# Attention probabilities of the first block: transposed by a float32 matmul with diag(1/sum) in place of a DMA, and a longer search for the order of the instructions

## The chip, the core and the metric

The kernel runs on one core of one Trainium2 chip. The metric is the device time of one execution in microseconds (us). The core has five engines with a queue each: TensorE (PE; its weight loads are listed apart as PEld), VectorE (DVE), ScalarE (ACT), GpSimd (POOL) and SyncE (SP), which here issues all transfers of the 16 DMA engines.

## What is computed

```python
# q, k, v: (4 batches, 12 heads, 448 positions, 64), float32
scores = q @ k.T / sqrt(64), causal mask
attn = exp(scores - max); attn = attn / (sum(attn) + 1e-9)
x = (attn @ v), heads side by side          # (1792, 768)
h = x @ w_in                                # w_in (768, 2048), float64
g = h * sigmoid(1.702 * h)
out = g @ w_out                             # w_out (2048, 768), float64
```

The inputs w_in and w_out are float64, 12.6 MB each. Results are float32.

## The kernel before

**Numbers in two halves.** Nearly every operand of a matmul is held as two float16 numbers, a high part and a remainder, and each product is three matmuls (high x high, high x remainder, remainder x high). The helper `scaled` makes a high part (L472 on ScalarE, L474 on VectorE), `rest` the remainder (L477, VectorE only). The weights are read as raw float64 words and made float32 by integer operations in `to_f32` (L566, L574, L588, L599), scaled by the largest column norm (`gram`, `gram_max` at L628, `norm_scale` at L439 to L453) and then split into halves by `split`, into `wib` (w_in, 8 slices) and back into `wob` (w_out, 16 pieces).

**Blocks and units.** Each batch of 448 positions is 7 chunks of 64 queries and is cut into a block of 4 chunks and a block of 3, so there are 8 blocks. A block has 6 units, each of two heads side by side: the 128 partitions are 64 queries of either head. In batch 0 the q and k of six units are float32 and turned by TensorE with an identity (`turn`, L866, `k_unit32`, `q_unit32`), so their scores are float32 matmuls. For each chunk `chunk` takes scores from PSUM, masks them and finds the maximum (L1085, VectorE), and ScalarE takes the exponential and the sum (L1099) into the tile `z`. GpSimd or VectorE adds 1e-9 (L1157), VectorE takes the reciprocal (L1163), and `p_pair` writes z times 1/sum as high part and remainder into `p16`. When all chunks of the unit are there, one DMA (L1173) transposes all of `p16` into `PT`, 128x128 at a time, and `pv` (L1191) multiplies with v. After every second unit the result is split into `xT`.

**The MoE part.** `moe(n)` runs over 8 slices of w_in (`h_slice`): matmuls of xT and wib into one of three PSUM buffers `ps_h`, tanh (L1282), product (L1287), split into `gT`. Then `out_tile` multiplies 128 rows of gT with w_out (L1325) and stores them. The matmuls of a slice come in two halves, over units 0 to 2 and 3 to 5.

**Order.** Nothing runs in the order of the source. `add` collects each operation with the tiles that it reads and writes, its cost on each engine that may run it (the first engine named is preferred, another takes it when it has nothing else ready), and a due time. `order` simulates the engines, sorts again and again with random noise on the finishing times, keeps the best, and the instructions are issued in that order. Each engine's queue then runs strictly in its order.

Of the kernel before, what the change touches and what calls it, by code (L numbers as in the profile page):

```python
# [11 lines left out]
F32 = mybir.dt.float32  # L12
# [3 lines left out]
ALU = mybir.AluOpType  # L16
# [10 lines left out]
TUNE = dict(  # L27
    large=2,
    raw=(['W11', 'W11', 'V1', 'V1', 'W13', 'W15', 'W9', 'V0'], ['W11', 'W13', 'W15', 'V1', 'W15', 'V0', 'V0', 'V1']),
    tiny=True,  # L30
    win=(2, 4),
    slack=5.13,
    cuts={0: (0, 4, 7), 1: (0, 4, 7), 2: (0, 4, 7), 3: (0, 4, 7)},
    wi=(-21.7, 11.6),
    wo=(38.54, 116.08),
# [16 lines left out]
    wi2=2.63,  # L52
    dv0=-29.57,
    early=3,
)

SEED = 2
# [2 lines left out]
class Ops:  # L60
# [24 lines left out]
    def add(self, costs, fn, r=(), w=(), prio=0.0, dma=0.0):  # L85
        deps = set()
        for key in r:
            if key in self.wrote:
                deps.add(self.wrote[key])
        for key in w:  # L90
            if key in self.wrote:
                deps.add(self.wrote[key])
            deps.update(self.read.get(key, ()))
        me = len(self.ops)
        for key in r:
            self.read.setdefault(key, []).append(me)
        for key in w:
            self.wrote[key] = me
            self.read[key] = []
        deps.discard(me)  # L100
        self.ops.append((costs, fn, sorted(deps), prio, dma))

    ROUNDS, STEPS, SPREAD = 300, 6, (0.0, 0.0, 1.0, 3.0, 8.0)

    def order(self):
        rnd = Random(SEED)
# [188 lines left out]
def act(n, psum=False, ap=0, acc=0, rate=0.833):  # L295
    return {"ACT": (rate * n + (52 if psum else 94) + 93 * (ap + acc)) / 1e3}


def dve(n, ap=0, rate=1.042):
    return {"DVE": (rate * n + 68 + 61 * ap) / 1e3}  # L300
# [7 lines left out]
def pool(n, rate=1.885):  # L308
    return {"POOL": (rate * n + 220) / 1e3}
# [3 lines left out]
def kernel(  # L313
# [11 lines left out]
    B, H, S, D = q.shape  # L325
    DM, DFF = w_in.shape
    P = 128
# [19 lines left out]
    def bufs(n, shape, dt, name, pool=cp):  # L347
        return [pool.tile(shape, dt, name=f"{name}{i}") for i in range(n)], Ring(n)
# [14 lines left out]
    PT, PT_r = bufs(2, [P, NPT, 2, P], F16, "PT")  # L363
# [4 lines left out]
    p16, p16_r = bufs(2, [P, NPT, 2, P], F16, "p16")  # L368
# [8 lines left out]
    ps_h, ps_h_r = bufs(3, [P, 512], F32, "ps_h", pp)  # L377
# [7 lines left out]
    add = ops.add  # L385
# [14 lines left out]
    def by(e):  # L400
        return nc.gpsimd if e == "POOL" else nc.vector
# [7 lines left out]
    def halves(out, lhsT, rhs, start, stop):  # L409

        for o in range(0, P, 64):
            nc.tensor.matmul(out[o : o + 64], lhsT[:, o : o + 64], rhs, start=start, stop=stop)  # L412
# [56 lines left out]
    def scaled(e, dst, src, sc):  # L469

        if e == "ACT":
            nc.scalar.activation(out=dst, in_=src, func=AF.Copy, scale=sc)  # L472
        else:
            nc.vector.tensor_scalar(out=dst, in0=src, scalar1=sc, scalar2=None, op0=ALU.mult)  # L474

    def rest(dst, src, sc, hi):
        nc.vector.scalar_tensor_tensor(out=dst, in0=src, scalar=sc, in1=hi, op0=ALU.mult, op1=ALU.subtract)  # L477
# [355 lines left out]
    ident = cp.tile([P, P], F32, name="ident")  # L833
    ident_keys = ["ident"]
# [190 lines left out]
    def q_unit(n, u, prio):  # L1025
        b, c0, c1 = blocks[n]
        if f32(b, u):
            return q_unit32(n, u, prio)
        ni = c1 - c0
        if u % 2 == 0:  # L1030
            q_pair(n, u, prio)
        t, m = qT_r.next(), u % 2
        stale[t] = True
        add(
            Ops.turned(2 * ni),
            lambda e: nc.sync.dma_start_transpose(out=qT[t][:, : 2 * ni], in_=q16[:, m * 256 * ni : (m + 1) * 256 * ni]),
            [("q16", m, g) for g in range(4)], [("qT", t)], prio - TUNE["tr"], dma=2 * Ops.ROWS * ni,
        )
        return (qT[t][:, : 2 * ni].rearrange("p (c g) t -> p g c t", g=2), ("qT", t)) + bst[b]["c", n]
# [65 lines left out]
    def z_of(i):  # L1105
        return zt[:, z_at[i] : z_at[i] + i // 2 + 1]

    def z_keys(i):
        return [("z", e) for e in range(z_at[i], z_at[i] + i // 2 + 1)]

    def p_pair(i, pi, at, r, r_key, prio):
# [13 lines left out]
            zs + [r_key] + keys[0], keys[1], prio,  # L1125
        )

    def unit(n, u, prio):
        b, c0, c1 = blocks[n]
        ni = c1 - c0  # L1130
        w = 64 * ni
        qt, qt_key, c, c_key = q_unit(n, u, prio - TUNE["dq"])
        pi = PT_r.next()


        places = [(i, J) for i in range(c0, c1) for J in range(i // 2 + 1)]
        if c0 == 0:
            places.sort(key=lambda x: x[1])
        where = {x: at for at, x in enumerate(places)}
        vt, v_keys = bst[b]["v16", u]  # L1140
        vb = u % 2
        ps = ps_v[:, vb]
        pp_i = p16_r.next()
        for i0 in range(c0 - c0 % 2, c1, 2):
            run = range(max(i0, c0), min(i0 + 2, c1))
            ls, l_key = col("l", 3, 2)
            rs, r_key = col("r", 3, 2)
            joint = [run] if sum(64 * (i + 1) for i in run) <= 512 else [[i] for i in run]
            got = [x for y in joint for x in scores_of(n, u, y, qt, qt_key, prio)]
            for a, i in enumerate(run):  # L1150
                chunk(i, *got[a], c, c_key, ls[:, a : a + 1], (l_key, a), prio)
            ln = len(run)
            ls, rs = ls[:, :ln], rs[:, :ln]
            l_keys = [(l_key, a) for a in range(ln)]
            add(
                tiny(),
                lambda e, ls=ls: by(e).tensor_scalar(  # L1157
                    out=ls, in0=ls, scalar1=1e-9, scalar2=2.0**-14, op0=ALU.add, op1=ALU.mult
                ),
                [], l_keys, prio,  # L1160
            )
            add(
                dve(6 * ln), lambda e, ls=ls, rs=rs: nc.vector.reciprocal(rs, ls), l_keys, [r_key], prio  # L1163
            )
            for a, i in enumerate(run):
                at = [where[i, J] for J in range(i // 2 + 1)]
                assert at == list(range(at[0], at[-1] + 1, at[1] - at[0] if at[1:] else 1))
                p_pair(i, pp_i, at, rs[:, a : a + 1], r_key, prio)
        ne = len(places)
        all_keys = [("PT", pi)]  # L1170
        add(
            Ops.turned(2 * ne),
            lambda e: nc.sync.dma_start_transpose(  # L1173
                out=PT[pi][:, :ne].rearrange("p a g t -> p (a g) t"),
                in_=p16[pp_i][:, :ne].rearrange("p a g w -> p (a g w)"),
            ),
            [("p16", pp_i, x, g) for x in range(ne) for g in range(2)], all_keys, prio - TUNE["tr"],
            dma=2 * Ops.ROWS * ne,
        )
        terms = []  # L1180
        for J in range((c1 - 1) // 2 + 1):
            first = max(c0, 2 * J)
            at = [where[i, J] for i in range(first, c1)]
            step = at[1] - at[0] if len(at) > 1 else 1
            assert at == list(range(at[0], at[-1] + 1, step))
            terms += [(J, first, slice(at[0], at[-1] + 1, step), gv, gp) for gv, gp in ((0, 0), (0, 1), (1, 0))]

        def pv(e):
            for t, (J, first, at, gv, gp) in enumerate(terms):
                for j in range(2):  # L1190
                    nc.tensor.matmul(  # L1191
                        ps[64 * j : 64 * j + 64, 64 * (first - c0) : w],
                        vt[:, gv, J, j, :],
                        PT[pi][:, at, gp, 64 * j : 64 * j + 64],
                        start=(t == 0),
                        stop=(t == len(terms) - 1),
                    )

        add(
            {"PE": sum((64 * (c1 - t[1]) / 2.4 + 5) for t in terms) / 1e3}, pv, v_keys + all_keys, [("PV", vb)], prio,  # L1200
        )
        if vb == 0:
            return
        pv_keys = [("PV", 0), ("PV", 1)]
        x = n % 2
        hi, lo = (xT[x][:, g, u - 1 : u + 1, :w] for g in range(2))
        keys = [[("xT", x, u - a, g) for a in range(2)] for g in range(2)]
        add(
            act(2 * w, psum=True),
            lambda e: scaled("ACT", hi, ps_v[:, :, :w], 2.0**-14),  # L1210
            pv_keys, keys[0], prio,
        )
        add(
            dve(2 * w),
            lambda e: rest(lo, ps_v[:, :, :w], 2.0**-14, hi),
            pv_keys + keys[0], keys[1], prio,
        )
# [236 lines left out]
```

## Time and profile before

| | |
|---|---|
| Runs | 614.44, 616.70, 617.17 us, median 616.7 |
| Profiled execution | 616.57 us |
| Its span, first to last instruction | 614.9 us |
| TensorE busy | 566.6 us, 92% |
| VectorE busy | 419.9 us, 68% |
| ScalarE busy | 359.5 us, 58% |
| GpSimd busy | 95.3 us, 16% |
| Mean granted TensorE clock | 0.975 |

Busy time is the time in which at least one instruction of the engine ran. A granted clock of 1.00 is TensorE's full 2.4 GHz, 0.50 is 1.2 GHz. A wait is put down to the operation that came last.

### The profile page before, as it was taken

The page shows a single profiled execution, that of the slowest core. Times are in us where ns is not written, and L with a number is a line of the kernel's source. Part 1 is how long each engine was busy: PE and PEld are TensorE (multiplying, and loading weights), DVE is VectorE, ACT ScalarE, POOL GpSimd, SP SyncE. Part 2 cuts the span into 40 slices and gives each one's busy share as a digit, 9 for nine tenths or more (in the row PEclk, how much of TensorE's full clock was granted, in tenths as well). Part 3 has the DMA queues.
Part 4 walks back from the last instruction along what each step waited for, and adds up shares of the span by engine and source line. Part 5 has one row for each costly group of instructions (what it writes and reads, how often), then busy time and mean ns, then how long its engine had stood idle before and what let it go on. Part 6 is the DMA issues. An engine that isn't in the chain of part 4 may idle for free.

```text
span 614.9 us, 22331 instructions
## 1 busy us (share of the span) xinstructions
PE 566.6 (92%) x9502; PEld 503.8 (82%) x9502; DVE 419.9 (68%) x1117; ACT 359.5 (58%) x830; POOL 95.3 (16%) x251
## 2 busy tenths in 40 slices
PE   4667689888999999999998999999999999999997
PEld 4455368766699989987897879998899999889986
DVE  4999999998978789996588885886685213102300
ACT  6987797788857666775677665875454123102310
POOL 2222210123212011421111422211010000000000
PEclk9786899999999999999999999999999999999999
DMA  9999999949699979899876998884870500000000
GB/s 302 234 276 278 307 186 306 254 133 197 104 163 166 162 127 152 150 172 193 154 114 129 143 176 164 137 120 95 152 126 3 100 15 2 2 27 29 3 27 27
DMA packets 226435, 86.18 MB, mean 140 GB/s; under 512 B 207136, under 2 KB 216096, under 8 KB 226336
## 3 DMA queue, kind: packets, MB, share of 16 engines
q1 hardware_dynamic: 226336, 84.76, 68.0%
q8 instruction: 74, 1.21, 0.8%
q14 instruction: 25, 0.20, 0.1%
HBM read 41.68 MB, written 5.51 MB: 77 GB/s over the span
## 4 chain that ended last, share of the span: by engine, by line
PE 55%; DVE 13%; ACT 4%; issue 3%; DMA 3%; POOL 2%; SPq 1%; DVEq 0%; ACTq 0%; POOLq 0%
PE ps_o L1325 25%; PE ps_h L412 25%; PE ps_v L1191 3%; PE ps_s L1062 3%; DVE p L477 2%; DMA qf<-in_q_dram 2%; DVE z L1085 2%; ACT z L1099 1%; DVE wob L477 1%; POOL cols L1227 1%; DVE ps_h L1287 1%; DVE p L474 1%; SPq L977 1%; DVE wob L599 1%; ACT waste L462 1%
## 5 line engine op out<-in xcount | busy, mean ns | idle before, releaser
L412 PE MATMUL ps_h<-xT,wib 128*64 128x256 f16 (+1 forms) x4608 | 239.7, 259 | 1.5 <-DVE gT L477 0.9
L1325 PE MATMUL ps_o<-wob,gT 128*64 128x384 f16 x2688 | 237.5, 326 | 3.8 <-DVE wob L477 2.1
L412 PEld LDWEIGHTS <-wib 128*64 128x64 f16 x4608 | 225.4, 110 | 6.7 <-issue 3.5
L1325 PEld LDWEIGHTS <-gT 128*64 128x64 f16 x2688 | 177.2, 110 | 39.1 <-issue 7.1
L1099 ACT ACTIVATE z<-z,cols 128x320 f32<-128x320 f32 (+5 forms) x168 | 83.8, 500 | 37.6 <-DVE cols L1085 31.3
L1287 DVE SCALAR_TENSOR_TENSOR ps_h<-t,ps_h 128x512 f32<-128x512 f32 (+1 forms) x64 | 40.0, 625 | 84.7 <-ACT t L1282 84.2
L477 DVE SCALAR_TENSOR_TENSOR p<-z,cols,p 128x384 f16<-128x384 f32 (+3 forms) x168 | 83.8, 526 | 1.7 <-ACT p L472 1.5
L1282 ACT ACTIVATE t<-ps_h,cols 128x512 f32<-128x512 f32 (+1 forms) x64 | 40.1, 626 | 44.9 <-PE ps_h L412 43.6
L1085 DVE CUSTOM_DVE_ANT_0 z<-ps_s,mask,cols 128x192 f32<-128x192 f32 (+5 forms) x126 | 55.9, 476 | 14.0 <-PE ps_s L1062 13.5
L472 ACT ACTIVATE ob<-ps_o,cols 128x384 f32<-128x384 f32 x25 | 14.4, 574 | 81.9 <-PE ps_o L1325 81.9
L472 ACT ACTIVATE p<-z,cols 128x256 f16<-128x256 f32 (+3 forms) x101 | 52.7, 554 | 15.6 <-DVE cols L1163 12.2
L1157 POOL TENSOR_SCALAR cols<-cols 128x2 f32<-128x2 f32 (+1 forms) x87 | 29.0, 333 | 202.9 <-ACT z L1099 201.5
L477 DVE SCALAR_TENSOR_TENSOR gT<-ps_h,gT 128x512 f16<-128x512 f32 (+1 forms) x64 | 39.6, 619 | 15.8 <-ACT gT L472 15.7
L472 ACT ACTIVATE gT<-ps_h 128x384 f16<-128x384 f32 (+1 forms) x57 | 30.7, 538 | 25.0 <-DVE ps_h L1287 25.0
L1062 PE MATMUL ps_s<-kT,qT 128*64 128x64 f16 (+4 forms) x504 | 39.5, 273 | 3.9 <-DVE cols L1085 3.2
L1191 PEld LDWEIGHTS <-v 128*64 128x64 f16 x864 | 40.3, 112 | 2.9 <-issue 0.6
L1191 PE MATMUL ps_v<-PT,v 128*64 128x192 f16 (+3 forms) x864 | 41.9, 241 | 0.0
L412 PE MATMUL ps_s<-kT,qT 128*64 128x128 f32 (+6 forms) x168 | 29.9, 476 | 4.8 <-DVE cols L1085 3.4
L1099 ACT ACTIVATION_READ_ACCUMULATOR z<-z,cols 128x1 f32 x168 | 31.6, 188 | 0.0
L1062 PEld LDWEIGHTS <-qT 128*64 128x64 f16 x504 | 24.6, 110 | 7.3 <-issue 4.8
L412 PE MATMUL ps_o<-wob 128*64 128x128 bf16 x384 | 18.4, 244 | 8.8 <-DVE wob L599 5.1
L474 DVE TENSOR_SCALAR p<-z,cols 128x128 f16<-128x128 f32 (+2 forms) x67 | 25.7, 408 | 1.0
(91 smaller groups left out, 537.5 us busy)
## 6 DMA issues: line engine op xcount, KB each, us to landing
wob<-in_moe_w_in_dram SPq DMA_DIRECT2D x16, 768.0 KB, 6.6
wob<-in_moe_w_out_dram SPq DMA_DIRECT2D x9, 768.0 KB, 7.2
vraw<-in_moe_w_out_dram SPq DMA_DIRECT2D x7, 768.0 KB, 5.1
out_dram<-ob SPq DMA_DIRECT2D x28, 192.0 KB, 2.5
vraw<-in_v_dram SPq DMA_DIRECT2D x12, 384.0 KB, 5.5
kf<-in_k_dram SPq DMA_DIRECT2D x36, 112.0 KB, 3.4
qf<-in_q_dram SPq DMA_DIRECT2D x48, 64.0 KB, 3.2
qf<-in_q_dram SPq DMA_DIRECT2D x48, 48.0 KB, 3.1
```

The lines of the kernel that those rows point to most:

```text
L412: nc.tensor.matmul(out[o : o + 64], lhsT[:, o : o + 64], rhs, start=start, stop=stop)
L472: nc.scalar.activation(out=dst, in_=src, func=AF.Copy, scale=sc)
L474: nc.vector.tensor_scalar(out=dst, in0=src, scalar1=sc, scalar2=None, op0=ALU.mult)
L477: nc.vector.scalar_tensor_tensor(out=dst, in0=src, scalar=sc, in1=hi, op0=ALU.mult, op1=ALU.subtract)
L1062: nc.tensor.matmul(ps[64 * j : 64 * j + 64], qt[:, g, i - c0, 64 * j : 64 * j + 64], kt[:, : i + 1, 64 * j : 64 * j + 64], start=(g == 0), ...
L1085: lambda e: nc.vector.tensor_tensor_reduce(out=z[:, :w], in0=ps, in1=mask[:, S - w :], scale=c, scalar=3.0e38, op0=ALU.add, op1=ALU.min, a ...
L1099: lambda e: nc.scalar.activation(out=z[:, :w], in_=z[:, :w], func=AF.Exp, bias=m, scale=-1.0, accum_out=l),
L1157: lambda e, ls=ls: by(e).tensor_scalar(out=ls, in0=ls, scalar1=1e-9, scalar2=2.0**-14, op0=ALU.add, op1=ALU.mult),
L1191: nc.tensor.matmul(ps[64 * j : 64 * j + 64, 64 * (first - c0) : w], vt[:, gv, J, j, :], PT[pi][:, at, gp, 64 * j : 64 * j + 64], start=(t ...
L1282: lambda e: nc.scalar.activation(out=th, in_=ph, func=AF.Tanh, scale=ts[:, sl : sl + 1]),
L1287: lambda e: nc.vector.scalar_tensor_tensor(out=ph, in0=th, scalar=1.0, in1=ph, op0=ALU.add, op1=ALU.mult),
L1325: nc.tensor.matmul(po[64 * j : 64 * j + 64, :OH], gT[:, f, gg, 64 * r : 64 * r + 64], wo_pair(f, gw, nh), start=(f == 0 and gg + gw == 0), ...
```

## The change

For the blocks named in `pet`, here only block 0 (batch 0, chunks 0 to 3), `p_pair` and the transposing DMA are not used. In their place, for each pair of chunks: a product of the identity with 1/sum gives a diagonal matrix for each chunk, in the place of `p16` (GpSimd or VectorE); float32 matmuls with z as the stationary operand and the diagonal as the moving one write z transposed and already scaled to a `ps_h` buffer (2 tiles for the first pair of chunks, 4 for the second); ScalarE or VectorE takes the high part from PSUM into `PT`, VectorE the remainder. `PT` is tracked in four parts. Apart from that, the search of `order` makes 1500 passes, not 300, with noise of 0, 0.5, 1 or 2, not 0, 0, 1, 3 or 8.

```diff
+    pet=(0,),
 )
...
-    ROUNDS, STEPS, SPREAD = 300, 6, (0.0, 0.0, 1.0, 3.0, 8.0)
+    ROUNDS, STEPS, SPREAD = 1500, 6, (0.0, 0.5, 1.0, 2.0)
...
+    def p_turned(run, pi, pp_i, where, rs, r_key, prio):
+
+        ln = len(run)
+        tiles = sorted((where[i, J], J, a, i) for a, i in enumerate(run) for J in range(i // 2 + 1))
+        p0, nt = tiles[0][0], len(tiles)
+        assert [t[0] for t in tiles] == list(range(p0, p0 + nt)) and 2 <= nt <= 4
+        diag = p16[pp_i][:, p0 : p0 + 2].rearrange("p a g w -> p (a g w)").bitcast(F32)
+        diag = diag.rearrange("p (a w) -> p a w", w=P)[:, :ln]
+        diag_keys = [("p16", pp_i, x, g) for x in (p0, p0 + 1) for g in range(2)]
+        add(
+            {**pool(ln * P), **dve(ln * P)},
+            lambda e: by(e).tensor_tensor(
+                out=diag,
+                in0=ident.unsqueeze(1).to_broadcast([P, ln, P]),
+                in1=rs.unsqueeze(2).to_broadcast([P, ln, P]),
+                op=ALU.mult,
+            ),
+            [r_key] + ident_keys, diag_keys, prio,
+        )
+        hb = ps_h_r.next()
+        ps = ps_h[hb][:, : nt * P]
+
+        def mm(e):
+            for at, J, a, i in tiles:
+                halves(ps[:, (at - p0) * P : (at - p0 + 1) * P], z_of(i)[:, J], diag[:, a], True, True)
+
+        add(
+            {"PE": nt * (4 * P / 2.4 + 150) / 1e3},
+            mm,
+            diag_keys + [k for i in run for k in z_keys(i)], [("H", hb)], prio,
+        )
+        ps3 = ps.rearrange("p (a w) -> p a w", w=P)
+        hi, lo = (PT[pi][:, p0 : p0 + nt, g] for g in range(2))
+        part = 2 * (p0 > 0)
+        add(
+            {**act(nt * P, psum=True), **dve(nt * P)},
+            lambda e: scaled(e, hi, ps3, 1.0),
+            [("H", hb)], [("PT", pi, part)], prio,
+        )
+        add(
+            dve(nt * P),
+            lambda e: rest(lo, ps3, 1.0, hi),
+            [("H", hb), ("PT", pi, part)], [("PT", pi, part + 1)], prio,
+        )
+
     def unit(n, u, prio):
...
+            if n in TUNE["pet"]:
+                p_turned(run, pi, pp_i, where, rs, r_key, prio)
+                continue
             for a, i in enumerate(run):
...
                 p_pair(i, pp_i, at, rs[:, a : a + 1], r_key, prio)
         ne = len(places)
-        all_keys = [("PT", pi)]
-        add(
+        all_keys = [("PT", pi, x) for x in range(4)]
+        if n not in TUNE["pet"]:
+          add(
             Ops.turned(2 * ne),
             lambda e: nc.sync.dma_start_transpose(
```

## Rows read from the trace of the kernel before

**Rows 1.** The page: busy us, share of the span, instructions of each engine.
```profile
PE 566.6 (92%) x9502; PEld 503.8 (82%) x9502; DVE 419.9 (68%) x1117; ACT 359.5 (58%) x830; POOL 95.3 (16%) x251
```

**Rows 2.** Busy time of each engine in three stages.
```profile
core 0: us, PE busy (x) PEld busy (x) DVE busy (x) ACT busy (x) POOL busy (x), PEclk, DMA share, GB/s
15.00:75.00 60.00, 39.68 (x526) 30.86 (x525) 59.10 (x150) 48.75 (x103) 14.04 (x30) 0.77 1.08 273
75.00:180.00 105.00, 93.25 (x1497) 74.88 (x1496) 100.53 (x224) 85.20 (x168) 22.42 (x50) 0.98 0.86 195
180.00:615.00 435.00, 427.01 (x7411) 391.76 (x7406) 253.48 (x727) 215.97 (x546) 54.36 (x151) 1.00 0.59 103
```

**Rows 3.** The chain that ended last, around 120 us: start us, us, what.
```profile
119.98 0.97 DVE wob L599
```

**Rows 4.** VectorE's groups up to 90 us: count | busy us, mean ns | idle before.
```profile
L477 DVE SCALAR_TENSOR_TENSOR p<-z,cols,p 128x256 f16<-128x256 f32 x12 | 5.4, 479 | 0.0
L477 DVE SCALAR_TENSOR_TENSOR p<-z,cols,p 128x128 f16<-128x128 f32 x12 | 3.8, 346 | 0.0
L477 DVE SCALAR_TENSOR_TENSOR xT<-ps_v,xT 128x512 f16<-128x512 f32 x3 | 2.0, 678 | 0.0
L474 DVE TENSOR_SCALAR p<-z,cols 128x256 f16<-128x256 f32 x5 | 1.7, 348 | 0.0
L474 DVE TENSOR_SCALAR kT<-ps_o 128x256 f32<-128x256 f32 x3 | 1.2, 411 | 0.1
L474 DVE TENSOR_SCALAR p<-z,cols 128x128 f16<-128x128 f32 x4 | 0.9, 276 | 0.0
```

**Rows 5.** GpSimd's costliest wide group over the span.
```profile
L1020 POOL TENSOR_SCALAR q<-q 128x512 f16<-128x512 f16 x18 | 13.8, 767 | 7.7 <-DVE q L477 5.3 <-ACT q L472 2.2
```

**Rows 6.** Timeline of VectorE and GpSimd, two places: start us, us, what.
```profile
125.57 0.74 DVE L477 SCALAR_TENSOR_TENSOR q<-qf,cols,q 128x512 f16<-128x512 f32 x1
...
171.35 1.10 DVE L477 SCALAR_TENSOR_TENSOR q<-qf,cols,q 128x512 f16<-128x512 f32 x1
...
126.39 1.32 POOL L1020 TENSOR_SCALAR q<-q 128x512 f16<-128x512 f16 x1 [1.18 <-DVE q L477]
...
171.29 0.62 POOL L1020 TENSOR_SCALAR q<-q 128x512 f16<-128x512 f16 x1
```

**Rows 7.** ScalarE's groups up to 90 us.
```profile
L472 ACT ACTIVATE p<-z,cols 128x256 f16<-128x256 f32 x7 | 3.4, 496 | 1.4 <-DVE cols L1163 1.4
L472 ACT ACTIVATE p<-z,cols 128x128 f16<-128x128 f32 x8 | 2.8, 396 | 1.3 <-DVE cols L1163 1.3
L472 ACT ACTIVATE xT<-ps_v 128x512 f16<-128x512 f32 x3 | 1.8, 590 | 0.6 <-PE ps_v L1191 0.6
```

**Rows 8.** TensorE's groups up to 90 us.
```profile
L412 PE MATMUL ps_s<-kT,qT 128*64 128x256 f32 x24 | 5.8, 540 | 0.0
L412 PE MATMUL ps_s<-kT,qT 128*64 128x128 f32 x24 | 4.0, 378 | 0.0
```

**Rows 9.** Busy time in one stage of 15 us, columns as in rows 2.
```profile
60.00:75.00 15.00, 8.33 (x128) 6.20 (x128) 14.95 (x32) 9.99 (x16) 4.49 (x8) 0.89 1.12 312
```

**Rows 10.** Landing of the six transposes from 15 to 82 us; SP's waits there.
```profile
DMA to landing us min/median/max: 4.2/6.6/9.5
...
SPq L1173 <- DVE cols L1163: 4.5, 1, 4.5
```

**Rows 11.** Timeline of SP and TensorE at the end of block 0: start us, us, what.
```profile
73.68 4.46 SPq L1173 DMA_TRANSPOSE PT<-p  x1
...
63.37 3.12 PE L412 MATMUL ps_h<-xT,wib 128*64 128x256 f16 x54
81.91 0.66 PE L1191 MATMUL ps_v<-PT,v 128*64 128x256 f16 x12
84.92 1.47 PE L412 MATMUL ps_h<-xT,wib 128*64 128x256 f16 x18
```

**Rows 12.** VectorE's costliest group from 90 to 180 us.
```profile
L477 DVE SCALAR_TENSOR_TENSOR wob<-wob,cols 128x768 f16<-128x768 f32 x16 | 16.2, 1010 | 1.2 <-ACT wob L472 1.2
```

## Prediction

> **What bounds the kernel now.** I read the busy shares first, then the span cut into stages, then the chain that ended last. Over the span TensorE is busy 92% and VectorE 68% [rows 1], so the first thought is that only TensorE counts. The stages correct it [rows 2]. From 180 us to the end TensorE is busy 427.0 of 435 us, at a granted clock of 1.00: nothing is to be had there except by less matmul work. Of the 48.3 us in which it idles in all (614.9 - 566.6) some 40 lie before 180 us, and there VectorE is what is full: 59.1 of 60 us between 15 and 75, and 100.5 of 105 between 75 and 180. The chain agrees [rows 3]: around 120 us it runs through VectorE's L599, the conversion of the float64 weights. So the kernel has two parts: one of about 165 us that VectorE sets (ScalarE, at 48.8 of 60, close behind), and one that TensorE sets. TensorE's work in the second part is fixed, so the kernel ends earlier by what the first part gets shorter.
>
> The change acts on batch 0's first block, six units between 15 and 83 us.
>
> **Part 1: VectorE's work for the probabilities.** Each unit has four chunks, two of 128 and two of 256 columns after padding; block 1 has 384 and 512, so the forms of 128 and 256 up to 90 us are this block alone [rows 4]. The float16 remainders (`rest`) cost 3.8 + 5.4 = 9.2 us on VectorE, and 9 of the 24 high parts also went to VectorE, 0.9 + 1.7 = 2.6. All 11.8 us go. In their place each unit has two remainders out of PSUM, of 256 and 512 columns. The 512 one is like the xT remainder, 678 ns; 256 out of PSUM is nearest to the kT copy, 411 ns [rows 4]. Six units: 6 x 1.09 = 6.5 us. The twelve new high parts may go to either engine. If VectorE takes the same 9/24 as before, that is 4.5 x 0.545 = 2.5 us (411 and 678 ns again, the mean of both); if none 0, if all 6.5. I take 2.5, since ScalarE is as full as before. VectorE so far: 11.8 - 6.5 - 2.5 = 2.8 us less.
>
> **Part 2: the diagonals.** Twelve products of `ident` and 1/sum, 128x256 float32, which may go to GpSimd or VectorE. GpSimd is listed first and is busy 14 of the 60 us, so I take it. No wide float32 product on GpSimd is in the trace; the nearest is the 128x512 float16 copy of L1020, 767 ns in the mean [rows 5]. GpSimd's own time is hidden, but not what it does to VectorE. The same remainder of 128x512 (q) takes 0.74 us at 125.57, when GpSimd does nothing (it idles 1.18 us up to 126.39), and 1.10 us at 171.35, when L1020's copy began 0.06 us before it [rows 6]. So a wide operation there costs VectorE from nothing (it falls beside an operation that it does not hold) to the whole 0.77 us. I take 0.2 us for each, a good half of the 0.36 that [rows 6] show, since some will fall beside others: 2.4 us, bounds 0 and 9.2. Were they on VectorE, 12 remainders of 128x256 (479 ns) would be 5.7, within these bounds.
>
> The Trainium skill ("SBUF — State Buffer", Who interferes with whom) says that a VectorE instruction with two SBUF inputs and a GpSimd instruction that reads SBUF lock each other out entirely, the later one waiting for the end of the first. The two q remainders agree with it (0.74 against 1.10 us). By that rule each diagonal that starts first would cost VectorE its whole length, which is the slower rival below.
>
> Net on VectorE: 2.8 - 2.4 = **0.4 us less**; at best 5.3 (11.8 - 6.5, no high part and no collision), at worst 6.4 more (2.8 - 9.2).
>
> **Part 3: ScalarE.** It loses 15 high parts, 3.4 + 2.8 = 6.2 us, and gains 7.5 at no more than 0.59 us (590 ns for 512 columns out of PSUM, the wider of the two) = 4.4 us, or 7.1 if it takes all [rows 7]. So it has at best 1.8 us more room and at worst 0.9 less. I count it at nothing: VectorE's work covers it.
>
> **Part 4: TensorE.** 36 float32 tiles of 128x128, each as two halves. In the scores, a chunk of 256 columns keeps TensorE busy 5.8/6 = 0.97 us, one of 128 columns 4.0/6 = 0.67 [rows 8]: 0.30 us for each 128 columns and 0.37 to start. A unit is then 0.97 (two tiles) + 1.57 (four) = 2.54 us, six units 15.2 us at today's mixed clock. The idle 60 - 39.7 = 20.3 us between 15 and 75 covers it, 5.1 us stay, and what follows needs xT, which comes later. So nothing on the path. Without that cover it would be up to 15.2. The clock of 0.77 there [rows 2] comes with a TensorE that is busy two thirds of the time; if it rises as TensorE has more to do, the 15.2 shrink, which I do not count either. TensorE's queue is in order: behind a transpose that waits for its diagonal stand weight Gram matrices (`gram`) and the next head's `turn`, and VectorE's `gram_max` waits for those. The idle time covers a short wait.
>
> **Part 5: DMA.** Of 48 transposes six go. Each was 4.2 to 9.5 us from issue to landing, and in front of one SP waited 4.5 us, with w_in, q and k loads behind it [rows 10]. The queue gets freer and the DMA engines, at 1.08, too. But VectorE does not rest for want of data between 15 and 75 (0.9 us idle), so I count nothing for faster loads. What does get earlier is the end of the block. Its last transpose is issued at 73.68, its `pv` runs at 81.91, and the second halves of `h_slice` start at 84.92, after a first batch of 54 matmuls at 63.37 [rows 11]. In place of 8.2 us (73.68 to 81.91) stand a diagonal 0.77, matmuls 1.57, a high part 0.59 and a remainder 0.68: 3.6 us. So MoE matmuls can start at least 4.6 us sooner. What is late next is the weights: the 16 remainders of w_out cost VectorE 16.2 us after 90 us [rows 12] and out_tile needs them, so the earlier start is worth only what VectorE idles between 75 and 180, 4.5 us, part of it waits for gate results. I take half, **2.2 us**; bounds 0 and 4.5.
>
> **Part 6: the order.** No row prices the search. It can fill idle TensorE time: 11.8 us between 75 and 180 and some 8 after that [rows 2]. I take 15% of these 19.8, **3.0 us**; at best twice that, 6.0. It can also lose: the constants in `TUNE` stay, and an order that looks shorter need not be so on the chip. As the bound on that side I take the 2.7 us by which the three runs of the present kernel differ, for want of a nearer row.
>
> **Sum.** 0.4 + 2.2 + 3.0 = 5.6 us. The profiled execution took 616.57 us (span 614.9 and 1.7 around it), 0.1 below the median of the three runs, so the sum stands against either: 616.6 - 5.6 = **611.0 us**, 0.9% faster. With all bounds at their good ends 5.3 + 4.5 + 6.0 = 15.8 less (600.8), at their bad ends 6.4 + 0 + 2.7 = 9.1 more (625.7).
>
> **Rivals.**
> *Slower, by GpSimd's hold on VectorE.* Place: 15 to 75 us. Each of the 12 diagonals blocks VectorE for 0.77 us, 9.2 in all, against 2.8 saved: 6.4 more; with 2.2 given back by the earlier start, 616.6 + 6.4 - 2.2 = 620.8. It decides from about 0.42 us per diagonal ((2.8 + 2.2)/12), with no gain from the order. For it: VectorE has no rest there, and [rows 6]. Against it: GpSimd would have to hold VectorE longer than the 0.36 us of [rows 6], and at all twelve.
> *Slower, by the order.* Place: anywhere before 180 us. The old order was found with these same constants, the new one need not fit the chip as well. Parts 1 to 5 alone give 616.6 - 2.6 = 614.0; a loss of 2.7 there only brings back 616.7, and it decides from 5.7 on (619.7). I put it at 7: 621. Against it: an order has to be bad over 5.7 us where 40 are idle to choose from.
> *No change.* The diagonals eat VectorE's saving, and the earlier MoE start is given back at the w_out remainders, which end at the same time: 616.6 less 0.4 = 616.2. For it: VectorE's 59.1 of 60.
> *Much faster.* SP's freer queue also lets weight work move ahead, so the 6.7 us in which TensorE idles between 60 and 75 [rows 9] are won on top: 611.0 - 6.7 = 604.3. Against it: VectorE must have done that work too.
>
> **How the numbers follow.** A measurement of this kernel can tell about 0.5%, 3.1 us, from no change: faster is below 613.6, slower above 619.7. Forecast (606 to 613.5) 0.42, much faster 0.13, no change 0.25, GpSimd's hold 0.12, order 0.08. That makes faster 0.55, same 0.25, slower 0.20. The likeliest case alone reaches from 606 to 613.5; the range leaves out about a tenth at each end, 602 to 621.
>
> **What would show it.** After: 42 transposes; 12 GpSimd products of 0.6 to 0.9 us; the first block's remainders at 6 to 7 us on VectorE; TensorE busy some 52 of 60 us between 15 and 75, with more clock; the second halves of `h_slice` by about 80 us. I would be wrong if VectorE's remainders of two SBUF inputs grow longer beside the products, if VectorE begins to idle before 75 us behind TensorE, or if the saved time shows before 90 us and is gone at 165, when the last w_out remainder ends.

## The result, and the profile after

The changed kernel took 607.93 us (median of four runs, 605.32 to 609.27) against 616.28 for the kernel before: a ratio of 0.9856, 95% interval 0.9834 to 0.9879. That is 1.4% or 8.3 us faster; forecast were 5.6 us (611.0), within a range of 602 to 621. The profiled execution took 608.42 us, its span is 606.7. In the profile after, the lines of the unchanged code carry numbers 1 to 50 higher than before (L477 is L478, L412 is L413, L1325 is L1375); in the kernels of the experiments they move by a few more.

The same three stages as in [rows 2]:

```profile
core 0: us, PE busy (x) PEld busy (x) DVE busy (x) ACT busy (x) POOL busy (x), PEclk, DMA share, GB/s
15.00:75.00 60.00, 42.96 (x685) 34.03 (x685) 58.64 (x143) 49.15 (x106) 23.45 (x43) 0.94 0.88 257
75.00:180.00 105.00, 97.38 (x1642) 81.73 (x1640) 99.69 (x227) 88.90 (x174) 26.60 (x52) 1.00 0.82 193
180.00:607.00 427.00, 420.62 (x7266) 389.39 (x7262) 258.36 (x744) 211.66 (x535) 47.51 (x124) 1.00 0.58 103
```

TensorE is busy 3.3 us more between 15 and 75 and 4.1 us more between 75 and 180, at a higher clock; VectorE is as full as it was. (The DMA share adds up the times of all packets, so it can pass 1.) What this is worth is seen from how much of the MoE matmul work is done by 180 us. The two views below are of the changed kernel from 0 to 180 us, first the `h_slice` matmuls alone, then those of `out_tile`; the last two lines are the same of the kernel before:

```profile
core 0: us, PE busy (x), PEclk, DMA share, GB/s
0.00:180.00 180.00, 46.84 (x800) 0.98 0.85 221
...
0.00:180.00 180.00, 35.74 (x372) 0.98 0.85 221
...
0.00:180.00 180.00, 38.72 (x648) 0.91 0.94 230
...
0.00:180.00 180.00, 35.48 (x379) 0.91 0.94 230
```

Their groups over the whole span, from the page of the changed kernel:

```profile
L413 PE MATMUL ps_h<-xT,wib 128*64 128x192 f16 (+1 forms) x4608 | 247.1, 260 | 1.2 <-DVE gT L478 1.2
L1375 PE MATMUL ps_o<-wob,gT 128*64 128x384 f16 x2688 | 244.0, 326 | 1.6 <-DVE wob L478 1.4
```

By 180 us the kernel before had done 648 of the first kind and 379 of the second. One of the first costs 247.1/4608 = 0.054 us, one of the second 244.0/2688 = 0.091. So the changed kernel is 152 x 0.0536 - 7 x 0.0908 = 7.5 us of TensorE work ahead when TensorE becomes the bound, and the span is 8.2 us shorter. The gain was made before 180 us and kept.

VectorE, ScalarE, GpSimd and TensorE up to 90 us, the groups that answer to [rows 4, 5, 7, 8] or are new:

```profile
L478 DVE SCALAR_TENSOR_TENSOR wib<-wob,cols,wib 128x1536 f16<-128x1536 f32 x8 | 15.3, 1916 | 0.4 <-ACT wib L473 0.3
...
L478 DVE SCALAR_TENSOR_TENSOR PT<-ps_h,PT 128x512 f16<-128x512 f32 x6 | 4.1, 678 | 0.2 <-ACT PT L473 0.2
...
L478 DVE SCALAR_TENSOR_TENSOR PT<-ps_h,PT 128x256 f16<-128x256 f32 x6 | 2.5, 416 | 0.3 <-ACT PT L473 0.3
...
L1140 DVE TENSOR_TENSOR p<-ident,cols 128x256 f32<-128x256 f32 x1 | 0.4, 425 | 0.0
...
L473 ACT ACTIVATE PT<-ps_h 128x512 f16<-128x512 f32 x6 | 3.6, 595 | 0.3 <-PE ps_h L413 0.2
...
L473 ACT ACTIVATE PT<-ps_h 128x256 f16<-128x256 f32 x6 | 2.3, 384 | 0.1
...
L1140 POOL TENSOR_TENSOR p<-ident,cols 128x256 f32<-128x256 f32 x11 | 9.2, 833 | 7.9 <-DVE cols L1209 4.5 <-PE ps_o L867 3.4
...
L413 PE MATMUL ps_h<-p,z 128*64 128x128 f32 x144 | 10.4, 279 | 3.3 <-POOL p L1140 3.3
...
L413 PE MATMUL ps_s<-kT,qT 128*64 128x256 f32 x24 | 3.6, 379 | 0.0
```

The remainders cost VectorE 6.6 us, as forecast (6.5). All twelve high parts went to ScalarE; eleven diagonals went to GpSimd and one to VectorE. TensorE's 144 float32 records are the 36 tiles, 10.4 us at a clock of 0.94 where 15.2 had been worked out at 0.77. The scores show the same: 3.6 us for what took 5.8 [rows 8].

The end of the first block: the last `xT` remainder on VectorE, and TensorE's `h_slice` matmuls around it (start us, us, what), to be held against [rows 11]:

```profile
77.75 0.69 DVE L478 SCALAR_TENSOR_TENSOR xT<-ps_v,xT 128x512 f16<-128x512 f32 x1
...
76.38 1.18 PE L413 MATMUL ps_h<-xT,wib 128*64 128x256 f16 x17
78.69 1.48 PE L413 MATMUL ps_h<-xT,wib 128*64 128x256 f16 x24
```

Before, that remainder began at 84.92, so the block ends 7.2 us sooner. Of this lead, 3.0 us are left when the last w_out remainder begins, here first in the kernel before and then in the changed one:

```profile
163.99 1.01 DVE L477 SCALAR_TENSOR_TENSOR wob<-wob,cols 128x768 f16<-128x768 f32 x1
...
160.99 1.01 DVE L478 SCALAR_TENSOR_TENSOR wob<-wob,cols 128x768 f16<-128x768 f32 x1
```

### The profile page after: what moved, and what is told of

The parts are those of the page before. It is cut to its first block, busy times and chain, and to the rows that moved or that the text cites. A ratio compares the mean times of both kernels' runs of the same rounds, so it can differ in the third digit from the quotient of the medians.

```text
span 606.7 us, 22564 instructions
## 1 busy us (share of the span) xinstructions
PE 567.6 (94%) x9646; PEld 510.2 (84%) x9646; DVE 422.1 (70%) x1121; ACT 358.5 (59%) x826; POOL 101.9 (17%) x239
## 5 line engine op out<-in xcount | busy, mean ns | idle before, releaser
L413 PE MATMUL ps_h<-xT,wib 128*64 128x192 f16 (+1 forms) x4608 | 247.1, 260 | 1.2 <-DVE gT L478 1.2
L1375 PE MATMUL ps_o<-wob,gT 128*64 128x384 f16 x2688 | 244.0, 326 | 1.6 <-DVE wob L478 1.4
L413 PEld LDWEIGHTS <-wib 128*64 128x64 f16 x4608 | 229.4, 110 | 7.2 <-issue 2.9
L1375 PEld LDWEIGHTS <-gT 128*64 128x64 f16 x2688 | 179.4, 110 | 31.9 <-issue 4.1
L1100 ACT ACTIVATE z<-z,cols 128x320 f32<-128x320 f32 (+6 forms) x168 | 84.0, 501 | 48.4 <-DVE cols L1086 47.3
L1337 DVE SCALAR_TENSOR_TENSOR ps_h<-t,ps_h 128x512 f32<-128x512 f32 (+1 forms) x64 | 40.1, 626 | 85.5 <-ACT t L1332 84.9
L1332 ACT ACTIVATE t<-ps_h,cols 128x512 f32<-128x512 f32 (+1 forms) x64 | 40.2, 629 | 73.6 <-PE ps_h L413 68.2
L478 DVE SCALAR_TENSOR_TENSOR p<-z,cols,p 128x384 f16<-128x384 f32 (+3 forms) x144 | 73.9, 541 | 3.3 <-ACT p L473 2.5
L1086 DVE CUSTOM_DVE_ANT_0 z<-ps_s,mask,cols 128x320 f32<-128x320 f32 (+6 forms) x126 | 56.7, 479 | 11.5 <-PE ps_s L1063 10.8
L473 ACT ACTIVATE p<-z,cols 128x384 f16<-128x384 f32 (+3 forms) x82 | 44.6, 562 | 15.3 <-DVE cols L1209 8.2
L478 DVE SCALAR_TENSOR_TENSOR gT<-ps_h,gT 128x512 f16<-128x512 f32 (+1 forms) x64 | 39.4, 619 | 10.0 <-ACT gT L473 9.4
L473 ACT ACTIVATE gT<-ps_h 128x512 f16<-128x512 f32 (+1 forms) x54 | 29.4, 544 | 19.3 <-DVE ps_h L1337 19.0
L1021 POOL TENSOR_SCALAR q<-q 128x512 f16<-128x512 f16 (+1 forms) x28 | 19.4, 694 | 54.5 <-ACT q L473 47.4
L475 DVE TENSOR_SCALAR p<-z,cols 128x256 f16<-128x256 f32 (+3 forms) x62 | 25.1, 423 | 3.7 <-DMA PT<-p 2.6
L473 ACT ACTIVATE wob<-wob 128x768 f32<-128x768 f32 (+1 forms) x20 | 22.1, 1104 | 7.7 <-DMA wob<-in_moe_w_in_dram 7.0
```

What stands on the lines that cost most here:

```text
L1086: lambda e: nc.vector.tensor_tensor_reduce(out=z[:, :w], in0=ps, in1=mask[:, S - w :], scale=c, scalar=3.0e38, op0=ALU.add, op1=ALU.min, a ...
L1100: lambda e: nc.scalar.activation(out=z[:, :w], in_=z[:, :w], func=AF.Exp, bias=m, scale=-1.0, accum_out=l),
L1332: lambda e: nc.scalar.activation(out=th, in_=ph, func=AF.Tanh, scale=ts[:, sl : sl + 1]),
L1337: lambda e: nc.vector.scalar_tensor_tensor(out=ph, in0=th, scalar=1.0, in1=ph, op0=ALU.add, op1=ALU.mult),
L1375: nc.tensor.matmul(po[64 * j : 64 * j + 64, :OH], gT[:, f, gg, 64 * r : 64 * r + 64], wo_pair(f, gw, nh), start=(f == 0 and gg + gw == 0), ...
```

## The experiments

Two groups: seven kernels with another search, seed or transpose, each with an order of its own; and five that keep an order, so that one thing differs. All ratios are to the kernel before, with 95% intervals.

**Each part alone, and other seeds.** The seed only starts the noise of the search; the work is the same.

```diff
 # search only (seeds 2, 3), in the kernel before
-    ROUNDS, STEPS, SPREAD = 300, 6, (0.0, 0.0, 1.0, 3.0, 8.0)
+    ROUNDS, STEPS, SPREAD = 1500, 6, (0.0, 0.5, 1.0, 2.0)
 # matmul only (seeds 2, 3), in the changed kernel: the same edit backwards
 # other seeds
-SEED = 2
+SEED = 3          # or 4
```

> The kernel before with only the search changed (1500 passes, new noise); the transposes stay DMAs. Theory A (both parts matter, the prediction's terms: search 3.0, transposes 2.6): about 613, ratio 0.995. Theory B (the search is all of it): 608, ratio 0.986. Theory C (the transposes are all of it): 616, ratio 1.000.

> The changed kernel with the search as before (300 passes, old noise); only the transposes are changed. Theory A: 611 to 613, ratio 0.991 to 0.995. Theory B (search is all): 616, ratio 1.000. Theory C (the transposes are all): 608, ratio 0.986.

> The kernel before with seed 3 in place of 2 for the noise of the search: the same work in another order. It measures how far another order alone moves the time. If the differences of e1 and e2 are due to what was changed, this one lies within 0.3% of before (614.5 to 618.1); if an order is a draw of luck, it lies off by as much as 1%.

> The changed kernel with seed 3 in place of 2. If the gain belongs to the change it stays: 606 to 610, ratio 0.983 to 0.990. If seed 2 was a lucky order, 612 to 616.

> Search changed, transposes as DMAs, seed 3. With e3 (622.2, the old search at seed 3) it gives the search's worth a second time. Theory A (each part has a worth of its own, the rest is the draw of the order): about 616 to 619, since the old search had drawn well at seed 2. Theory D (a longer search finds more only when the transposes are matmuls): 622, as e3.

> Transposes changed, the old search, seed 3. Theory A: the matmuls alone are worth some 2.6 us against the same search and seed with DMAs (e3: 622.2), so 617 to 621. Theory D (with the old search the matmul transposes cost time, as e2 against before at seed 2): 625 or more.

> The changed kernel with seed 4. A third draw of the order beside 607.9 (seed 2) and 612.1 (seed 3). If the gain belongs to the change, the three lie below every order of the kernel with DMA transposes (615.9 to 624.9), so 605 to 613; it would be the better version of the two if it falls below 606.

| | old search, 300 | new search, 1500 |
|---|---|---|
| DMA transposes, seed 2 | 1 (the kernel before) | 0.9987 [0.9965, 1.0009] |
| DMA transposes, seed 3 | 1.0114 [1.0083, 1.0145] | 1.0125 [1.0093, 1.0157] |
| matmul transposes, seed 2 | 1.0083 [1.0052, 1.0113] | 0.9856 [0.9834, 0.9879] (the change) |
| matmul transposes, seed 3 | 0.9986 [0.9968, 1.0005] | 0.9940 [0.9920, 0.9959] |
| matmul transposes, seed 4 | | 0.9964 [0.9949, 0.9980] |

At seed 2 neither part alone gains anything: the search alone -0.1%, which cannot be told from nothing, the matmuls alone 0.8% slower. Together they gain 1.4%. Theories A, B and C all fail as sums. A seed alone moves the time as much as the change does: by 1.1% (old search) and 1.4% (new) with DMA transposes, by 1.0% (old) and 0.8% to 1.1% (new) with matmuls. Seed 3 of the changed kernel (612.1 us) lies where the expectation had put a lucky seed 2, and seed 4 (614.3) lies outside the 605 to 613 that it had if the gain belongs to the change. With DMA transposes the long search gave nothing at either seed (1.000 to 0.9987, 1.0114 to 1.0125). With matmuls it gave 2.3% at seed 2 and 0.5% at seed 3. Compared at the same seed and the new search, the matmuls gain 1.3% (seed 2) and 1.8% (seed 3); at the old search they lose 0.8% and gain 1.3%. The mean over the five orders with matmuls is 0.997, over the four with DMA transposes 1.006. So on the average of these draws the matmuls are 0.9% faster, but the four comparisons scatter from a loss of 0.8% to a gain of 1.8%, and a mean of four such numbers does not tell 0.9% from nothing. How much of the 1.4% belongs to the matmuls, to the search and to the draw is therefore not shown. Nor is it settled whether the longer search helps only with matmuls: theory D had the long search with DMA transposes at seed 3 about right (622 against 624.9), but the matmuls with the old search at seed 3 at 625 or more, where 615.8 was measured.

**TensorE's clock.** The kernel before, in its own order, with 36 more float32 tiles behind the first block's scores.

```diff
+            if c0 == 0:
+                for x in range(2 if run[0] == 0 else 4):
+                    halves(ps_h[2][:, x * P : (x + 1) * P],
+                        qt[:, x % 4].rearrange("p j w -> p (j w)"), kt[:, :P], True, True)
```

> The kernel before in its own order, unchanged, with as many extra float32 128x128 matmuls behind the first block's scores as the change adds (their result is used by nothing). The granted clock between 15 and 75 us should rise from 0.77 towards the 0.94 of the changed kernel. Theory E (the gain is TensorE's clock): 611 to 613. Theory A (the clock there is worth nothing, VectorE sets that stage): 616 to 619.

The ratio is 0.9996 [0.9980, 1.0012]. Its stage from 15 to 75 us (columns as above), the added matmuls in that stage, and two groups up to 90 us; last the same stage of the kernel with the matmul transposes alone at seed 2:

```profile
15.00:75.00 60.00, 40.12 (x647) 33.99 (x645) 57.60 (x147) 47.56 (x100) 13.31 (x29) 0.87 1.06 266
```
```profile
L412 PE MATMUL ps_h<-kT,qT 128*64 128x128 f32 x120 | 9.9, 298 | 0.0
```
```profile
L412 PE MATMUL ps_h<-kT,qT 128*64 128x128 f32 x144 | 11.8, 294 | 0.0
...
L412 PE MATMUL ps_s<-kT,qT 128*64 128x256 f32 x24 | 4.9, 464 | 0.0
```
```profile
15.00:75.00 60.00, 39.93 (x651) 32.93 (x652) 56.20 (x129) 47.18 (x96) 22.85 (x42) 0.91 0.87 244
```

The clock rises from 0.77 to 0.87, and TensorE takes 9.9 us more work in the stage (11.8 up to 90 us) while its busy time hardly moves (39.7 to 40.1 us). The time stays. So the matmuls fit into idle time, as the prediction had counted, and most of what they cost comes back by the clock, which it had left uncounted. A clock of 0.87 alone gains nothing, so theory E finds no support; the changed kernel's 0.94 was not reached here, but the kernel with the matmuls alone has 0.91 in that stage and is 0.8% slower than before.

**The transposes without the wait, and with it.** The changed kernel in its own order. First six DMA transposes are put back, 8 of the former 12 tiles each, from a part of `p16` that GpSimd sets to zero once at the start, into a part of `PT` that this block does not use; nothing in the block waits for them. Then a matmul of one column ahead of `pv` reads what they wrote.

```diff
+        def last():
+            rest(lo, ps3, 1.0, hi)
+            if p0:
+                nc.sync.dma_start_transpose(
+                    out=PT[pi][:, 6:10].rearrange("p a g t -> p (a g) t"),
+                    in_=p16[pp_i][:, 6:10].rearrange("p a g w -> p (a g w)"))
 # only in the second kernel, at the start of pv
+            if n in TUNE["pet"]:
+                nc.tensor.matmul(ps[:64, :1], vt[:, 0, 0, 0, :], PT[pi][:, 9, 1, :1], start=True, stop=True)
```

> The changed kernel in its own order, with a DMA transpose of 8 tiles (of a part of p16 set to zero) issued after each unit's last remainder, and a matmul ahead of the unit's product with v that reads what it wrote and whose result is overwritten. So the wait for a transpose is back, the rest stays. Theory A (the end of the first block earlier is part of the gain): it ends some 5 us later and the time goes up by 2 to 4 us, 610 to 612. Theory F (the wait is worth nothing): 608.

> As x5 (621.3), the changed kernel in its own order with the six DMA transposes of 8 tiles each, but nothing waits for what they write. It parts what x5 lost: the wait at the product with v, or the transposes themselves on SP's queue and the DMA engines. Theory A (the wait): 607 to 609. Theory G (the transposes' own load): 615 or more.

Without the wait the ratio is 0.9924 [0.9895, 0.9954], with it 1.0058 [1.0034, 1.0082]. So the transposes' own load costs 0.7% (0.9856 to 0.9924, about 4.2 us) and the wait another 1.3% (about 8.3 us). The stage from 15 to 75 us without the wait, with VectorE's two longest waits in it (us in total, times, longest); then the stage with the wait, and two of its waits from 15 to 180 us:

```profile
15.00:75.00 60.00, 41.11 (x671) 33.88 (x669) 55.59 (x139) 47.07 (x103) 21.28 (x42) 0.91 1.05 269
```
```profile
DVE cols L629 <- PE ps_o L413: 1.5, 2, 1.3
DVE wob L575 <- DMA wob<-in_moe_w_in_dram: 1.1, 1, 1.1
```
```profile
15.00:75.00 60.00, 38.40 (x599) 31.74 (x597) 49.69 (x127) 41.02 (x97) 21.01 (x34) 0.91 0.93 243
```
```profile
PE ps_v L1250 <- DMA PT<-p: 17.0, 4, 4.7
...
DVE cols L629 <- PE ps_o L413: 5.1, 2, 2.9
```

Without the wait the DMA engines are back at 1.05 (0.88 in the changed kernel, 1.08 before), and VectorE, which was full, does 3.0 us less work by 75 us (55.6 against 58.6). The waits that its trace lists there rise from 0.8 to 3.9 us, 1.1 of them directly for a load of w_in and 1.5 for Gram matrices from TensorE. That is the expected 607 to 609 missed, and theory G in a smaller size. Whether the DMA engines or SP's queue is what costs is not parted: the shortest of the six transposes holds SP for 1.2 us (below, shortest, median and longest in ns), where a load of w_in issued at 47.35 takes 0.38.

```profile
L1179 SPq DMA_TRANSPOSE PT<-p x6: 1232/1716/4331, 30.0 to 72.7; - x6
```

What this kernel does not bring back is SP's wait for the data of a transpose. In the kernel before, SP stood in front of five of the six transposes between 15 and 82 us, 17.0 us in all, with the loads behind them in its queue; here its listed wait in front of them is 2.7 us. The lines are of the kernel before, the fifth stands in [rows 10]:

```profile
SPq L1173 <- DVE cols L628: 4.5, 1, 4.5
...
SPq L1173 <- DVE cols L1085: 3.8, 1, 3.8
SPq L1173 <- ACT p L472: 3.0, 1, 3.0
...
SPq L1173 <- ACT wob L566: 1.2, 1, 1.2
```

With the wait TensorE stands 17.0 us in its queue, which is in order, for transposes that land 5.1 to 8.3 us after their issue; the Gram matrices behind it are late, VectorE waits 5.1 us for them, and by 75 us it has done 8.9 us less than in the changed kernel. The last `xT` remainder begins at 89.66 instead of 77.75, 11.9 us later where some 5 were expected, and the time is 621.3 where 610 to 612 were. This order was made for a kernel without the wait, so 8.3 us is what the wait costs where the order does not know of it; the kernel before, with all of the wait, takes less time than this one.

**Where the diagonals are made.** The changed kernel in its own order, with all twelve on VectorE, or on ScalarE.

```diff
+        def make_diag(e):
+            if e == "ACT":
+                for a in range(ln):
+                    scaled(e, diag[:, a], ident, rs[:, a : a + 1])
+                return
+            by(e).tensor_tensor(out=diag, ...)
...
-            ops.ops[i][1](e)
+            ops.ops[i][1]("ACT" if i in diag_ops else e)    # or "DVE"
```

> The changed kernel in its own order, with all twelve diagonals on VectorE (11 were on GpSimd). VectorE gets 11 x 0.43 = 4.7 us more between 15 and 75 us and is rid of GpSimd's hold, which lengthened its w_in remainders by 8 x 0.1 = 0.8 us. Theory A (VectorE sets the stage): 3 to 4 us slower, 611 to 612. Theory H (VectorE's work there is covered): 608.

> The changed kernel in its own order, with all diagonals on ScalarE as 24 products of 128 columns at 0.38 us, 9.1 us more there, where it idles 10.9 of 60. It takes GpSimd's hold off VectorE and costs VectorE nothing. Theory A (VectorE sets the stage, ScalarE has that room): 606 to 609. Theory I (ScalarE is as tight as VectorE): 612 or more.

On VectorE the ratio is 0.9876 [0.9856, 0.9897], on ScalarE 0.9840 [0.9817, 0.9862]; both intervals overlap that of the changed kernel (0.9834 to 0.9879). The groups up to 90 us, on VectorE and then on ScalarE:

```profile
L479 DVE SCALAR_TENSOR_TENSOR wib<-wob,cols,wib 128x1536 f16<-128x1536 f32 x8 | 14.4, 1805 | 0.0
...
L1145 DVE TENSOR_TENSOR p<-ident,cols 128x256 f32<-128x256 f32 x12 | 5.0, 418 | 0.0
```
```profile
L479 DVE SCALAR_TENSOR_TENSOR wib<-wob,cols,wib 128x1536 f16<-128x1536 f32 x8 | 14.5, 1811 | 0.6 <-ACT wib L474 0.6
...
L474 ACT ACTIVATE p<-ident,cols 128x128 f32<-128x128 f32 x24 | 8.3, 397 | 0.5 <-DVE cols L448 0.5
```

With the diagonals off GpSimd the w_in remainders take 1805 and 1811 ns, with them on GpSimd 1916. So GpSimd's hold on VectorE is real and costs 8 x 0.105 = 0.8 us there. In the changed kernel's timeline it is three of the eight that are longer, 2.05, 2.13 and 2.05 us, each with a diagonal that began before it and was not over; the other five took 1.81 to 1.83. The last line is a GpSimd operation of one column that began beside the second of them:

```profile
23.43 1.31 POOL L1140 TENSOR_TENSOR p<-ident,cols 128x256 f32<-128x256 f32 x1 [0.20 <-DVE cols L1209]
...
50.53 0.61 POOL L1140 TENSOR_TENSOR p<-ident,cols 128x256 f32<-128x256 f32 x1
...
54.25 0.61 POOL L1140 TENSOR_TENSOR p<-ident,cols 128x256 f32<-128x256 f32 x1 [0.81 <-DVE cols L1209]
...
24.30 2.05 DVE L478 SCALAR_TENSOR_TENSOR wib<-wob,cols,wib 128x1536 f16<-128x1536 f32 x1
...
50.62 2.13 DVE L478 SCALAR_TENSOR_TENSOR wib<-wob,cols,wib 128x1536 f16<-128x1536 f32 x1
54.43 2.05 DVE L478 SCALAR_TENSOR_TENSOR wib<-wob,cols,wib 128x1536 f16<-128x1536 f32 x1
...
51.11 1.70 POOL L447 TENSOR_SCALAR cols<-cols 128x1 int32<-128x1 int32 x1
```

The same comparison over all of VectorE's groups up to 90 us comes to some 1.6 us.

Moving 4.6 us of diagonals onto VectorE (5.0 against 0.4) cost 0.2% (about 1.2 us), between theory H (608) and theory A (611 to 612). It cannot be told from nothing, and its interval reaches to some 3 us. Less the hold, VectorE got 3.0 to 3.8 us more, so how much of a microsecond of VectorE work in this stage is passed on is not settled. The version on ScalarE, 607.11 us as theory A had it (606 to 609), is the fastest median of all, by less than can be told from the changed kernel; as that one lies in the same range, this decides nothing.

**One measure for all of them.** MoE work done by 180 us is counted as above (0.054 and 0.091 us for one matmul of each kind):

| kernel | slice, out matmuls by 180 us | MoE work, us | span, us | sum |
|---|---|---|---|---|
| before | 648, 379 | 69.2 | 614.9 | 684.1 |
| search only, seed 2 | 702, 370 | 71.2 | 612.6 | 683.8 |
| search only, seed 3 | 612, 332 | 63.0 | 625.6 | 688.6 |
| before, seed 3 | 612, 356 | 65.1 | 618.9 | 684.0 |
| matmul only, seed 2 | 683, 360 | 69.3 | 616.7 | 686.0 |
| matmul only, seed 3 | 648, 378 | 69.1 | 612.6 | 681.7 |
| the change | 800, 372 | 76.7 | 606.7 | 683.4 |
| the change, seed 3 | 756, 369 | 74.0 | 609.0 | 683.0 |
| the change, seed 4 | 684, 384 | 71.5 | 612.5 | 684.0 |
| more matmuls | 643, 372 | 68.2 | 613.7 | 681.9 |
| transposes, no wait | 747, 360 | 72.7 | 609.4 | 682.1 |
| transposes and wait | 630, 330 | 63.7 | 619.8 | 683.5 |
| diagonals on VectorE | 756, 368 | 73.9 | 606.9 | 680.8 |
| diagonals on ScalarE | 826, 372 | 78.1 | 605.4 | 683.5 |

Spans run over 20 us, the sums over 8; without one kernel (search only, seed 3) spans over 14, sums over 5. So in all of them the time is mostly set by how far the MoE matmuls are when TensorE becomes full.

## Why the prediction was right, and where it was not

Right: the direction, the stage in which the gain is made, and that TensorE's new work is hidden by its idle time (the kernel with more matmuls shows it). Its price was 10.4 us, not 15.2, and TensorE was busy 43.0 of 60 us, not some 52: with the clock at 0.94 its other work got shorter too, which part 4 had left out. The transposed remainders were sized right, 6.6 against 6.5 us. The first block ends 7.2 us sooner, where at least 4.6 had been said, and most of that lead is used up by the w_out remainders, 3.0 us of it being left. Against the bound of 4.5 us, with 2.2 taken, that 3.0 is the nearest that a trace gives; no run parts it from the DMA's share.

Mis-sized, part 2: GpSimd's hold was put at 2.4 us. One of the prediction's own signs of being wrong came: remainders of two SBUF inputs grew longer beside the products. But on the w_in remainders that is 0.8 us (some 1.6 over all groups), and the two versions that avoid it do not differ measurably from the change. VectorE's net saving comes to 11.8 - 6.6 - 0.4 - 0.8 = 4.0 us, or 3.2 with the 1.6, and not 0.4: the 2.5 us of high parts that were put on VectorE went to ScalarE. What such a saving is worth in time is open.

Failed, part 5: "I count nothing for faster loads", because VectorE had no idle time between 15 and 75 us. Putting two thirds of the transposes back without any wait cost about 4.2 us. A full VectorE did not mean that the DMA engines, at 1.08, and SP's queue were out of the way: in an order made for less traffic VectorE's waits rise to 3.9 us when the transposes come back. Part 5 also read SP's wait as 4.5 us in front of one transpose; the same view has 17.0 us in front of five. No run prices that wait by itself.

Failed as a sum, part 6: the search was priced at 3.0 us of its own. Alone it gave 0.8 us at seed 2, which cannot be told from nothing, and at seed 3 nothing. Its worth with the matmuls ranges from 0.5% to 2.3%. So the total came out near the forecast with this term not standing as it was argued, and the DMA term missing: that the sum came so near is in part luck.

The rivals: the hold of GpSimd is there, at 0.8 to 1.6 us over eleven diagonals, far from the 0.42 us per diagonal from which it decides. The loss by the order did not come at seed 2, but seed 4 of the changed kernel (0.9964) is only 0.4% faster than before, so a draw is worth nearly as much as the change; with that seed the gain would have been 2.2 us.

## What to carry to other kernels

Where an order is found by a noisy search, one order against one order measures the draw as well as the change: run some seeds of both, since here a seed alone was worth up to 1.4%. Find the moment at which the last bound takes over and count the final engine's work that is done by then; that one number followed the time of nearly all fourteen kernels. A resource that is full beside another full one (here the DMA engines and SP's queue beside VectorE) is not free because nobody is seen to wait for it.

## What was not expected of the hardware

More float32 matmuls in a stage where TensorE came and went cost it hardly any busy time: 30 of 36 tiles fell into the stage, 9.9 us, and raised it from 39.7 to 40.1 of 60 us, while the granted clock went from 0.77 to 0.87 and the other matmuls got shorter (scores of 256 columns 464 ns each, not 540).

And GpSimd's hold on VectorE can be sized. The three w_in remainders above began with 0.44, 0.52 and 0.43 us of a diagonal to go (for the second 50.53 + 0.61 - 50.62), and took 0.24, 0.32 and 0.24 us longer than the 1.81 us without: each time what was left, less 0.2 us. The q remainder of [rows 6] fits as well, with 0.56 us left (171.29 + 0.62 - 171.35) and 0.36 us longer. By the rule of the Trainium skill that the prediction cites ("SBUF — State Buffer", Who interferes with whom), the later one waits for the end of the first; the traces agree but for these 0.2 us, and what they are is open. The hold goes the other way too: the GpSimd operation of one column at 51.11 took 1.70 us and ended 0.06 us after the VectorE remainder beside it, where a like one at 44.54 took 0.19.
